# Two layers of attention and token-mixing MLP on one core: a PSUM tile of its own for each of the three accumulators of a pair

## The chip, the cores and the metric

The kernel runs on one core of one Trainium2 chip. The metric is the device time of one execution in microseconds (us). Three runs of the kernel before gave 2514.11, 2517.06 and 2518.97 us; their median is 2517.06 us.

## The reference, cut to what matters

Two kinds of layer alternate, each twice, on x of 2048 tokens by 512 channels, all in float32:

```python
x = x + _A_ref(_layernorm(x), wq, wk, wv, wo)     # attention, 32 query heads, one key and value head
x = x + _B_ref(_layernorm(x), w1, b1, w2, b2)     # token mixing
...
def _B_ref(x, w1, b1, w2, b2):
    h = _layernorm(x)                             # (S, D)
    u = _gelu(einsum("bsd,sf->bdf", h, w1) + b1)  # (D, F), F = 1792
    y = einsum("bdf,fs->bds", u, w2) + b2         # (D, S)
    return y.transpose                            # (S, D)
```

The change touches only the second matrix product of the last token-mixing layer: y = W2ᵀu for all 2048 tokens, with a sum over the 1792 rows of w2.

## The kernel before

Every product is made in float32 precision out of three passes: each operand is split in a high part (a rounded copy, made by ScalarE at L1465 in `split`) and a low part (the rest, made by VectorE at L1466), and TensorE multiplies high by high, high by low and low by high, in this order (`split_terms`). So the first and second matmul of a triple read only the high part of the left operand, the third needs the low part.

The program is one stream: attention of layer 0, mixing of layer 0, attention of layer 1, mixing of layer 1. In the last stage, `pairs` (from the last product with w1 to the end), the output is made in 8 pairs of token tiles, a pair being two tiles of 128 tokens. u lies in SBUF as 14 tiles of 128 rows. For two pairs (`WHOLE_PAIR`) the product is made plainly: four quarter blocks of 7 × 3 matmuls of 512 columns. For the other six (`ENTRY_PAIR` once, then `PAIR` five times) a 2 by 2 block product is made with seven block products instead of eight (a scheme after Strassen and Winograd). Each block is 7 × 3 matmuls of 256 columns (L1579 in `block`). The left operand of a block is a 128-column block of w2 or a sum of such blocks, made by VectorE (`outer_sum`, L1507 and L1512); the right operand is a half of u (B11, B21, B22) or a sum of halves (T1 to T4) made earlier.

The seven blocks of a pair, by their place j, with the accumulator (X, Z or Y) each one adds to and the parts of x that are updated ("evicted") when it ends:

```python
PAIR = (
    ("A11", "B11", "X", True, ("11b",)), ("A12", "B21", "Z", True, ("11",)),
    ("S2", "T2", "X", False, ("12b",)), ("S1", "T1", "Y", True, ("22b",)),
    ("S3", "T3", "X", False, ("22",)), ("S4", "B22", "Y", False, ("12",)),
    ("A22", "T4", "X", False, ("21b",)),
)
```

So X takes blocks 0, 2, 4 and 6, Z takes block 1 alone, Y takes blocks 3 and 5. An accumulator goes on growing after it has been read: X is read after block 0, then block 2 adds to it. The eviction is one VectorE instruction that reads PSUM and adds into x in SBUF: L1588 (with the bias) or L1592 (without).

PSUM has eight banks of 512 float32 a partition. The pool "sc" has three tiles of two banks (`bank2`); "ac0" and "ac1" are one bank each (`bank`). Before the change, a pair takes one two-bank tile, X is its first half and Z its second half, that is, the bank beside it; Y is a single bank. The framework records waits by tile: an instruction that writes a part of a tile waits for the earlier readers of that tile, whichever part they read.

The order of instructions is the order in which the code is written, engine by engine. For block n of the whole stage, `split_pair(n + 2)` comes first (ScalarE's high part, VectorE's low part, of the left operand for two blocks later), then `beside` (outer sums of the next pair from place 3 on, the loads of w2 for a later pair on SP's queue at place 5; in the entry pair the split of T1 at places 0 to 3), then the matmuls of block n, then its eviction. So in VectorE's queue each eviction of block n stands behind the low part for block n + 2 and behind one outer sum.

Of the kernel before, what the change touches and what calls it, by code (L numbers as in the profile page):

```python
# [68 lines left out]
NPAIR, NWHOLE = NKT // 2, 2  # L69
# [20 lines left out]
def kernel(  # L90
# [26 lines left out]
    def bank2(name):  # L117
        return ps.tile([P, 2, QB], F32, tag="sc", bufs=3, name=name)

    def bank(i, name):  # L120
        return ps.tile([P, QB], F32, tag=f"ac{i % 2}", name=name)
# [973 lines left out]
    class Mixer:  # L1095
# [442 lines left out]
        def pairs(self):  # L1538

            n = 0  # L1540
            for q, table in enumerate(PAIRS):
                both = bank2(f"py_{q}")
                banks = {"X": both[:, 0], "Z": both[:, 1], "Y": bank(q, f"pyy_{q}")}
                for j, entry in enumerate(table):
                    self.split_pair(n + 2)
                    self.beside(q, j, n)
                    self.block(q, n, banks[entry[2]], *entry)
                    n += 1
# [354 lines left out]
```

## Time and profile before

| what | value |
|---|---|
| runs | 2514.11, 2517.06, 2518.97 us; median 2517.06 us |
| the profiled execution | 2514.75 us, span of the trace 2513.0 us |
| VectorE busy | 1623.0 us, 65% of the span |
| ScalarE busy | 2127.2 us, 85% |
| DMA | mean 57 GB/s |
| stage `pairs` | first matmul of L1579 at 2352.7 us, last eviction at 2509.33 us |
| first block of the entry pair | starts at 2391.61 us |

Times in the trace are us from the start of the span. A row of the timeline has the start, the length, the engine, the line, the operation, what it writes and what it reads, how many equal instructions in a row it holds and, in brackets, how long the engine sat idle before it and what ended that idle time. PE is TensorE's matmul, PEld its weight load, DVE is VectorE, ACT is ScalarE. The tile of X and Z is named py, that of Y pyy; rA holds w2's blocks, rS a sum of them, w a split left operand; t, u, kst and qs hold right operands.

### The profile page before, as it was taken

To read this page: it belongs to the slowest core of one execution; us is meant where nothing else is said; L and a number is where in the kernel's file an instruction comes from. 1 tells how busy PE (TensorE), PEld (TensorE's weight loads), DVE (VectorE), ACT (ScalarE), POOL (GpSimd) and SP (SyncE) were. 2 spreads that over 40 slices of the span, in tenths; PEclk is the share of its full clock that TensorE was granted. 3 is DMA by queue.
4 is the path that set the end of the run, shared out by engine and by line. 5 is a ranking of instruction groups with operands and counts; after the bars stand their busy time and mean duration, and the time that the engine had idled before them with its cause. 6 is when DMAs were issued, how large, how long until landed. Compare 5 with 4: busy or idle time off the path is not lost. (4 is left out here: it accounts for less than half of the span.)

```text
span 2513.0 us, 42927 instructions
## 1 busy us (share of the span) xinstructions
PE 2488.0 (99%) x16536; PEld 1252.8 (50%) x16536; DVE 1623.0 (65%) x2587; ACT 2127.2 (85%) x2390; POOL 147.5 (6%) x235
## 2 busy tenths in 40 slices
PE   9999999999999999999999999999999999999998
PEld 6444344444444444588863443444444444446888
DVE  6565566667766776564545664666677667765776
ACT  6999999999999999653349999999999999995532
POOL 5000000000000000141000000000000000002200
PEclk9999999999999999999999999999999999999999
DMA  3221201110111111144413211111111111102442
GB/s 116 75 66 41 65 29 39 33 40 31 39 31 39 32 40 31 44 113 147 125 57 118 67 39 48 32 40 31 39 32 42 33 40 32 40 27 68 116 141 65
DMA packets 168684, 143.63 MB, mean 57 GB/s; under 512 B 17650, under 2 KB 132368, under 8 KB 167952
## 3 DMA queue, kind: packets, MB, share of 16 engines
q1 hardware_dynamic: 168464, 140.72, 18.9%
q8 instruction: 135, 2.21, 0.4%
q14 instruction: 85, 0.70, 0.1%
HBM read 97.67 MB, written 26.22 MB: 49 GB/s over the span
## 5 line engine op out<-in xcount | busy, mean ns | idle before, releaser
L939 ACT ACTIVATE p<-sc 128x1024 f32<-128x1024 f32 x1444 | 1405.7, 1049 | 62.6 <-PE sc L929 61.4
L937 DVE COPY p<-sc 128x1024 f32<-128x1024 f32 x604 | 739.1, 1224 | 523.3 <-PE sc L929 438.4
L945 PE MATMUL acc<-p,vaug 128*32 128x512 f32 x8192 | 1000.1, 599 | 0.4 <-DVE q L548 0.4
L929 PE MATMUL sc<-qs,kst 51*128 51x512 f32 x4096 | 683.9, 432 | 6.8 <-SPq L647 2.6
L939 ACT ACTIVATE p<-p 128x1024 f32<-128x1024 f32 x604 | 655.8, 1086 | 14.2 <-DVE p L937 9.2
L929 PEld LDWEIGHTS sc<-qs,kst 51*128 51x128 f32 x4096 | 338.2, 184 | 559.5 <-ACT p L939 387.4
L945 PEld LDWEIGHTS acc<-p,vaug 128*32 128x32 f32 x8192 | 219.0, 109 | 489.4 <-issue 473.1
L1224 PE MATMUL pu<-hb,w 128*128 128x512 f32 x792 | 209.4, 406 | 0.0
L1224 PEld LDWEIGHTS pu<-hb,w 128*128 128x128 f32 x792 | 140.9, 188 | 57.6 <-issue 32.0
L1211 POOL TENSOR_TENSOR w<-w1r,w 128x256 fp32r<-128x256 f32 x86 | 69.4, 815 | 1581.9 <-ACT w L1209 1581.2
L1627 PE MATMUL py<-u,w 128*128 128x512 f32 x672 | 154.8, 390 | 0.0
L1627 PEld LDWEIGHTS py<-u,w 128*128 128x128 f32 x672 | 125.7, 188 | 26.1
L865 DVE RECIPROCAL o<-o 128x128 f32<-128x128 f32 x120 | 113.3, 944 | 9.0 <-DMA o<-ev 9.0
L906 PE MATMUL po<-wo,hl 128*128 128x512 f32 x360 | 100.2, 412 | 0.1
L1615 ACT CAST w<-w2r 128x896 fp32r<-128x896 f32 x32 | 30.0, 943 | 76.8 <-PE py L1627 69.5
L1465 ACT CAST w<-rA 128x896 fp32r<-128x896 f32 x44 | 41.3, 942 | 62.3 <-PE py L1579 44.4
L847 DVE COPY ev<-acc 128x512 f32<-128x512 f32 x64 | 43.7, 682 | 62.7 <-PE acc L945 62.7
L435 PE MATMUL pq<-hT,wq 128*128 128x512 f32 x312 | 81.1, 403 | 0.0
L906 PEld LDWEIGHTS po<-wo,hl 128*128 128x128 f32 x360 | 62.6, 188 | 33.7 <-issue 15.9
L1224 PE MATMUL pu_l<-hb,w 128*128 128x512 f32 x336 | 77.1, 389 | 0.0
L1209 ACT CAST w<-w1r 128x256 fp32r<-128x256 f32 x86 | 34.3, 406 | 48.0 <-PE pu_l L1224 16.6
L1616 DVE TENSOR_TENSOR w<-w2r,w 128x896 fp32r<-128x896 f32 x32 | 37.1, 1159 | 52.2 <-ACT w L1615 52.2
(224 smaller groups left out, 1628.1 us busy)
## 6 DMA issues: line engine op xcount, KB each, us to landing
w1r<-in_B_w_dram SPq DMA_DIRECT2D x224, 128.0 KB
qs<-qd SPq DMA_DIRECT2D x384, 64.0 KB
qd<-q SPq DMA_DIRECT2D x64, 256.0 KB
o<-ev SPq DMA_DIRECT2D x128, 128.0 KB
w2r<-in_B_w_dram SPq DMA_DIRECT2D x32, 448.0 KB
rA<-in_B_w_dram SPq DMA_DIRECT2D x32, 448.0 KB
x<-in_A_x_dram SPq DMA_DIRECT2D x16, 256.0 KB
hd<-hT SPq DMA_DIRECT2D x2, 2048.0 KB
```

Source lines behind the costliest of these rows:

```text
L435: yield nc.tensor.matmul(out, a, c, start=(k == 0), stop=(k == len(terms) - 1))
L847: nc.vector.tensor_copy(ev, acc)
L865: nc.vector.reciprocal(o[:, 1, c], o[:, 1, c])
L906: nc.tensor.matmul(po, a, c, start=(k == 0), stop=(k == 3 * len(parts) - 1))
L929: nc.tensor.matmul(sc[:, j, :], kst[kt // 4][rows, kt % 4 * P : (kt % 4 + 1) * P], qs[i % NQ][rows, j0 // 2, :], start=True, stop=True,)
L937: nc.vector.tensor_copy(pt, sc)
L939: nc.scalar.activation(pt, sc, AF.Exp, scale=0.25)
L945: nc.tensor.matmul(self.acc[i][c : c + 32, :], vaug[:, kt].rearrange("p d k -> p (d k)"), pt[:, j, :], start=(kt == 0), stop=(kt == NKT - ...
L1211: eng.tensor_tensor(w[:, 1], raw, f32(w[:, 0]), op=ALU.subtract)
L1224: nc.tensor.matmul(pu, a, c, start=(start and k == 0), stop=(stop and k == 5))
L1465: nc.scalar.copy(out[:, 0], src)
L1627: nc.tensor.matmul(py, a, d, start=(c == 0 and f == 0 and k == 0), stop=(c == 1 and f == NFH - 1 and k == 2),)
```

## The change

```diff
             for q, table in enumerate(PAIRS):
-                both = bank2(f"py_{q}")
-                banks = {"X": both[:, 0], "Z": both[:, 1], "Y": bank(q, f"pyy_{q}")}
+                banks = {key: bank2(f"py{key}_{q}")[:, 0] for key in ("X", "Z")[: 1 + (q >= NWHOLE)]}
+                banks["Y"] = bank(q, f"pyY_{q}")
```

X and Z each get a two-bank tile from the same pool of three and use the first bank of it. The two plain pairs, which have no Z, take one such tile as before. In the six other pairs two of the three tiles are in use at a time instead of one. As built, Z lies in bank 2 in all six pairs and X in banks 6, 4, 6, 4, 6, 4; before, X lay in banks 6, 2, 4, 6, 2, 4 and Z in the bank above each. Y keeps banks 0 and 1 in turn. No instruction is added, removed or moved on any engine; what differs is which semaphores some matmuls wait for, and up to what count.

On TensorE, in the pair with q = 4, the end of block 0 (left operand w_22, into X) and the start of block 1 (w_23, into Z) stand so before; a row is a line of code, an operation, the tile written, the tiles read, the size, and the semaphores waited for (DVE is VectorE's, Activation ScalarE's):

```order
L1579 MATMUL py_25115<-u_10_24020,w_22_25053 128x256 x3
L1579 MATMUL py_25115<-u_12_24022,w_22_25053 128x256 x3
L1579 MATMUL py_25115<-u_1_24011,w_23_25088 128x256 [waits DVE_49,Activation_49]
L1579 MATMUL py_25115<-u_1_24011,w_23_25088 128x256 x2
L1579 MATMUL py_25115<-u_3_24013,w_23_25088 128x256 x3
```

The same place after the change:

```order
L1579 MATMUL pyX_25117<-u_10_24020,w_22_25055 128x256 x3
L1579 MATMUL pyX_25117<-u_12_24022,w_22_25055 128x256 x3
L1579 MATMUL pyZ_25118<-u_1_24011,w_23_25090 128x256 [waits Activation_49]
L1579 MATMUL pyZ_25118<-u_1_24011,w_23_25090 128x256
L1579 MATMUL pyZ_25118<-u_1_24011,w_23_25090 128x256 [waits DVE_49]
L1579 MATMUL pyZ_25118<-u_3_24013,w_23_25090 128x256 x3
```

Block 1's first matmul no longer waits for VectorE; its third matmul, the first that reads a low part, does.

On TensorE, in the same pair, the end of block 2 (w_24, into X) and the start of block 3 (w_25, into Y) before:

```order
L1579 MATMUL py_25115<-t_5_24610,w_24_25117 128x256 x3
L1579 MATMUL py_25115<-t_6_24652,w_24_25117 128x256 x3
L1579 MATMUL pyy_25116<-u_0_24010,w_25_25142 128x256 [waits Activation_49]
L1579 MATMUL pyy_25116<-u_0_24010,w_25_25142 128x256 x2
L1579 MATMUL pyy_25116<-u_2_24012,w_25_25142 128x256 x3
```

And after:

```order
L1579 MATMUL pyX_25117<-t_5_24610,w_24_25120 128x256 x3
L1579 MATMUL pyX_25117<-t_6_24652,w_24_25120 128x256 x3
L1579 MATMUL pyY_25119<-u_0_24010,w_25_25145 128x256 [waits Activation_49]
L1579 MATMUL pyY_25119<-u_0_24010,w_25_25145 128x256
L1579 MATMUL pyY_25119<-u_0_24010,w_25_25145 128x256 [waits DVE_49]
L1579 MATMUL pyY_25119<-u_2_24012,w_25_25145 128x256 x3
```

Block 3 has gained a wait of its own for the low part of w_25. Before, that low part was covered by the wait at the start of block 2, which was for the eviction of block 1 (behind that low part in VectorE's queue); after, block 2's first matmul still waits for VectorE, in a row that reads alike, but up to a lower count: that of the eviction of block 0.

## The prediction

> **What bounds the kernel now.** I read the page first: which engine is busy, and how much of the span is left for a gain at all.
>
> ```profile
> span 2513.0 us, 42927 instructions
> PE 2488.0 (99%) x16536; PEld 1252.8 (50%) x16536; DVE 1623.0 (65%) x2587; ACT 2127.2 (85%) x2390; POOL 147.5 (6%) x235
> ```
>
> TensorE is busy for 99% of the span; it is the bound, and what can be won without taking matmuls away is the time in which it stands still. Next I asked for the one line that the change touches, L1579, and what its engine waited for before it.
>
> ```profile
> its engine sat idle before it (us, times) until:
>   issue: 8.9, 11
>   DVE x L1588: 5.7, 6
>   DVE x L1592: 3.6, 6
> ```
>
> The matmuls stood still 6 times until an eviction at L1588 had ended and 6 times until one at L1592 had: twelve waits, two in each of the six pairs that have a Z. (The 8.9 us of "issue" are weight loads standing beside the same waits, not further time.) To see where they lie I read the timeline of one whole pair, q = 4.
>
> ```profile
> 2430.61 1.09 DVE L1466 TENSOR_TENSOR w<-rA,w 128x896 fp32r<-128x896 f32 x1
> ...
> 2431.89 2.68 PE L1579 MATMUL py<-u,w 128*128 128x256 f32 x21
> 2432.74 0.48 DVE L1588 SCALAR_TENSOR_TENSOR x<-py,b2c,x 128x256 f32<-128x256 f32 x1
> 2433.14 1.08 DVE L1466 TENSOR_TENSOR w<-rA,w 128x896 fp32r<-128x896 f32 x1
> 2434.61 0.48 DVE L1588 SCALAR_TENSOR_TENSOR x<-py,b2c,x 128x256 f32<-128x256 f32 x1 [0.39 <-PE py L1579]
> 2434.67 0.94 ACT L1465 CAST w<-rS 128x896 fp32r<-128x896 f32 x1 [1.59 <-PE py L1579]
> 2435.24 2.76 PE L1579 MATMUL py<-u,w 128*128 128x256 f32 x21 [0.67 <-DVE x L1588]
> 2435.64 1.09 DVE L1466 TENSOR_TENSOR w<-rS,w 128x896 fp32r<-128x896 f32 x1 [0.54 <-ACT w L1465]
> 2438.04 0.42 DVE L1592 TENSOR_TENSOR x<-x,py 128x256 f32<-128x256 f32 x1 [1.31 <-PE py L1579]
> 2438.61 2.73 PE L1579 MATMUL py<-t,w 128*128 128x256 f32 x21 [0.61 <-DVE x L1592]
> 2441.18 2.68 PE L1579 MATMUL pyy<-u,w 128*128 128x256 f32 x21
> 2444.36 0.48 DVE L1588 SCALAR_TENSOR_TENSOR x<-pyy,b2c,x 128x256 f32<-128x256 f32 x1
> 2446.20 2.68 PE L1579 MATMUL pyy<-u,w 128*128 128x256 f32 x21
> 2446.88 0.41 DVE L1592 TENSOR_TENSOR x<-x,py 128x256 f32<-128x256 f32 x1
> 2448.72 1.59 PE L1579 MATMUL py<-kst,w 128*128 128x256 f32 x12
> 2451.22 2.68 PE L1579 MATMUL py<-u,w 128*128 128x256 f32 x21
> ```
>
> Blocks 0, 1 and 2 start at 2431.89, 2435.24 and 2438.61, block 3 (into Y) at 2441.18, the next pair at 2451.22. Between block 0 and block 1, and between block 1 and block 2, TensorE waits for an eviction; from block 3 on each starts as the one before ends, although evictions go on there too, because X and Y take turns.
>
> **The change part by part.**
>
> *The length of a block without a wait.* Blocks 3 to 6 take 2451.22 − 2441.18 = 10.04 us, 2.51 us each. I use starts, not the lengths in the rows: 2.68 us for a block that is followed after 2.51 us has its pipeline's end drawn in. For the same reason the idle times (0.67 and 0.61 us) are shorter than what a wait costs.
>
> *The first wait, block 1 on X's eviction, removed.* Block 1 could start at 2431.89 + 2.51 = 2434.40. The eviction starts 0.21 us after that, runs 0.48 us, and block 1 starts 0.15 us after its end, at 2435.24: 0.84 us lost. Block 1 writes into Z, which nobody is reading; only the shared tile makes it wait.
>
> *The second wait, block 2 on Z's eviction, removed.* Block 2 could start at 2435.24 + 2.51 = 2437.75, and starts at 2438.61: 0.86 us. Block 2 itself lasts 2.57 us from start to start, 0.06 us more than one that follows without a break. Together the three blocks take 9.29 us where 3 × 2.51 = 7.53 us would do: 1.76 us a pair. The idle rows say that the other pairs are alike: 3.6 us over 6 waits at L1592 is 0.60 each, and 5.7 us at L1588, less the longest (2.37 us, below), is 0.67 each over 5. So the five pairs of kind PAIR give 5 × 1.76 = 8.8 us.
>
> *The entry pair.* It waits longer:
>
> ```profile
> 2391.61 2.68 PE L1579 MATMUL py<-u,w 128*128 128x256 f32 x21
> 2394.37 1.08 DVE L1466 TENSOR_TENSOR w<-rA,w 128x896 fp32r<-128x896 f32 x1
> 2395.37 0.75 DVE L1466 TENSOR_TENSOR u<-t,u 128x256 fp32r<-128x256 f32 x2
> 2396.04 0.48 DVE L1588 SCALAR_TENSOR_TENSOR x<-py,b2c,x 128x256 f32<-128x256 f32 x1
> 2396.66 2.75 PE L1579 MATMUL py<-u,w 128*128 128x256 f32 x21 [2.37 <-DVE x L1588]
> 2402.59 2.68 PE L1579 MATMUL pyy<-u,w 128*128 128x256 f32 x21
> ```
>
> Here X's eviction starts only at 2396.04, since a low part and the split of T1 stand ahead of it on VectorE. Blocks 0 to 2 take 2402.59 − 2391.61 = 10.98 us, 3.45 us over 7.53. Without the first wait block 1 starts at 2394.12 and block 2 could start at 2396.63; it must still wait for X's eviction, 2396.04 + 0.48 + 0.15 = 2396.67, so 0.04 us of the gain stays behind. Of this pair I count 3.4 us.
>
> *What becomes late next.* Block 2 keeps its true wait, for the eviction of X after block 0. In the pair above that ended 2434.61 + 0.48 − 2431.89 = 3.20 us after block 0's start, 3.35 with the 0.15 to the next matmul; block 2 comes 5.02 us after it. Slack 1.67 us: hidden behind block 1. The waits added, on the third matmul of blocks 1 and 3 for a low part: that of block 1 ends at 2430.61 + 1.09 = 2431.70, before block 0 begins; that of block 3 (2435.64 + 1.09) ends 4.84 us after block 0's start, follows a cast at 2434.67 which waits for block 0's end and no later one, and is needed after 7.5 us. What such a wait costs when it is already met no row isolates; block 0 has one on its third matmul now, and its eviction starts 2434.61 − 2431.89 = 2.72 us after its start, against 2438.04 − 2435.24 = 2.80 for block 1, which has none. I take 0, and ± 0.02 us each, ± 0.2 us in all twelve, as bounds. Behind those waits only TensorE's own next matmuls are queued. Block 6 waits for block 4's eviction, which ends at 2447.29, 1.43 us before block 6 starts; block 5 for block 3's, which ends at 2444.84, 1.36 us before.
>
> *VectorE's share.* It gets the same work in less time.
>
> ```profile
> core 0: us, PE busy (x) PEld busy (x) DVE busy (x) ACT busy (x) POOL busy (x), PEclk, DMA share, GB/s
> 2391.40:2412.60 21.20, 18.22 (x149) 17.82 (x148) 18.21 (x28) 8.73 (x14) 0.00 (x0) 1.00 0.58 163
> 2431.90:2451.30 19.40, 18.12 (x150) 17.77 (x149) 14.67 (x19) 6.59 (x7) 0.00 (x0) 1.00 0.43 125
> ```
>
> A pair shrinks to 7 × 2.51 = 17.6 us. VectorE has 14.67 us in it: room. In the entry pair it has 18.21 us, more than 17.6 (durations of neighbours overlap by up to 0.1 us, so truly a little less): evictions will run late there, by up to 0.6 us, against slacks of 1.3 to 1.7, and the next pair has 2.9 us to make it up. I take no stall from it, and as a bound that half of this pair's gain, 1.7 us, is given back. The weights come at 125 GB/s with the DMA engines 43% busy; 10% more a second does not fill them. ScalarE has 6.59 us.
>
> *The end.* After the last matmul the eviction and the store remain as they are:
>
> ```profile
> 2509.33 0.48 DVE L1588 SCALAR_TENSOR_TENSOR x<-py,b2c,x 128x256 f32<-128x256 f32 x1 [2.08 <-PE py L1579]
> ```
>
> From this last eviction to the span's end 3.7 us stay, and so does everything ahead of 2391.61 us.
>
> *The sum.* 8.8 + 3.4 = 12.2 us off the profiled execution: 2514.75 − 12.2 = 2502.6, with a span near 2500.8. The profiled execution lies 2.3 us under the median of the three runs; against that, 2517.06 − 12.2 = 2504.9 us, my forecast. Bounds of the gain: 12.2 + 0.2 = 12.4 above, 12.2 − 0.2 − 1.7 = 10.3 below.
>
> Could an unbroken block be shorter than 2.51 us, so that more is to be won? The two plain pairs have matmuls of twice the width:
>
> ```profile
> 2372.10 9.96 PE L1579 MATMUL py<-u,w 128*128 128x512 f32 x42
> 2381.90 9.87 PE L1579 MATMUL pyy<-u,w 128*128 128x512 f32 x42
> ```
>
> There 42 matmuls of 512 columns take 9.80 us, 0.233 us each; half of that, 0.117 us for 256 columns, makes 2.45 us for 21, at the same granted clock of 1.00. I keep to 2.51, which blocks of this very kind show. The Trainium skill ("TensorE: Matmul & The Clock Gate", section "Back-to-back issue gap") gives 262 cycles for an isolated matmul of 256 columns, an estimated 2.29 us for 21 of them at its full clock of 2.4 GHz. The trace does not agree with it for this stream, in which each matmul has a weight load of its own. By that pace the waits would be estimated at 2.42 us a pair and 4.11 in the entry pair, 16.2 us in all.
>
> **The rivals.**
>
> *Only half goes.* Were the eviction of X after block 0 later than reckoned, block 2 would stall on it in place of Z's. Then about 0.86 us a pair stays, 12.2 − 6 × 0.86 = 7.0 us are won: 2510.1 us. For it: the entry pair is 0.04 us from this. Against: 1.67 us of slack in the other five.
>
> *Nothing comes of it.* The time is given back at another wait, later in each pair (blocks 4 to 6) or on a new tile: Z now draws on the same three tiles as X. That gives 2517.1 us. Against: Z's own first matmul waits for ScalarE alone, and X, in banks 6 and 4 by turns, never takes the tile that X had in the pair before.
>
> *Slower: VectorE becomes the bound.* Its place is the queue from block 3 on, where a low part, an outer sum and an eviction come in every 2.51 us. If its instructions grew longer once TensorE writes without a break, evictions would fall behind and blocks 4, 5, 6 would stall. From 17.6 us of VectorE work a pair, 20% over 14.67, the gain shrinks; from 19.3 us, 32% over, it turns. At 40%, 20.5 us a pair, the five pairs would lose 5 × 1.2 = 6 us: 2523 us. Against: the eviction at 2432.74 took 0.48 us with TensorE at work, the one at 2434.61 took 0.48 with TensorE standing.
>
> *Blocks that are faster too.* Were the 42 blocks held back by these waits in a way that no idle row shows, they could come down to the 2.45 us of the plain pairs: 42 × 0.06 = 2.5 us more, 14.7 us in all, 2502.4 us. Against: blocks 3 to 6 follow each other without a wait now and take 2.51. The isolated pace stated by the Trainium skill ("TensorE: Matmul & The Clock Gate", "Back-to-back issue gap") would carry this further, to an estimated 2500.9 us.
>
> **How the numbers follow.** Forecast 0.86, half 0.06, nothing 0.04, slower 0.03, faster blocks 0.01. The range follows the forecast's bounds, laid on the lowest and highest run: 2514.11 − 12.4 = 2501.7 and 2518.97 − 10.3 = 2508.7; the other cases, 0.14 together, may be left out. A measurement of this kernel can tell about 0.2%, 5 us, from no change. Faster by more than that: the forecast, the faster blocks, and half of the half case, 0.90; within it: the other half and "nothing", 0.07; slower: 0.03.
>
> **What would show it.** In the profile after: blocks 0 to 2 start 2.5 us apart in every pair; the idle rows of L1579 name L1588 and L1592 no more, but for some tenths of a us in the entry pair; a PAIR takes 17.6 us; VectorE's busy time is the same. I am wrong if a stall stands at block 2 (half), at blocks 4 to 6 with longer idle times until L1588 or L1592 (VectorE), or if unbroken blocks take other than 2.51 us.

## The result, and the profile after

The changed kernel took 2502.63 us (median of five runs, 2501.36 to 2506.12) against 2515.78 us for the kernel before (five runs, 2514.11 to 2518.97): a ratio of 0.995 with a 95% interval from 0.9936 to 0.9965, that is 13.15 us by the medians and 8.8 to 16.1 us by the interval. The forecast was 12.2 us. The profiled execution took 2502.08 us.

The page after, and under it the answer for line L1579 with its idle times:

```profile
span 2500.3 us, 42921 instructions
PE 2484.6 (99%) x16536; PEld 1251.9 (50%) x16536; DVE 1622.2 (65%) x2587; ACT 2127.2 (85%) x2390; POOL 148.2 (6%) x235
```

```profile
its engine sat idle before it (us, times) until:
who waited for it (us, times):
...
```

The counts of TensorE and VectorE are the same; the span is 12.7 us shorter. Under the heading of idle times there is nothing left: in the whole stage no matmul of L1579 finds its engine idle. The timeline of the pair q = 4, which the prediction showed before the change:

```profile
2426.22 2.68 PE L1579 MATMUL pyX<-u,w 128*128 128x256 f32 x21
2428.74 2.68 PE L1579 MATMUL pyZ<-u,w 128*128 128x256 f32 x21
2428.94 0.48 DVE L1588 SCALAR_TENSOR_TENSOR x<-pyX,b2c,x 128x256 f32<-128x256 f32 x1 [0.39 <-PE pyX L1579]
...
2431.26 2.65 PE L1579 MATMUL pyX<-t,w 128*128 128x256 f32 x21
2431.46 0.42 DVE L1592 TENSOR_TENSOR x<-x,pyZ 128x256 f32<-128x256 f32 x1 [0.40 <-PE pyZ L1579]
...
2433.75 2.68 PE L1579 MATMUL pyY<-u,w 128*128 128x256 f32 x21
...
2443.80 2.68 PE L1579 MATMUL pyX<-u,w 128*128 128x256 f32 x21
```

Block 1 starts 2.52 us after block 0, while X's eviction has not even begun (2428.94, 0.20 us later); block 2 starts before Z's eviction. Blocks 0 to 2 take 2433.75 − 2426.22 = 7.53 us in place of 9.29, the pair 17.58 in place of 19.33. In the entry pair:

```profile
2391.04 2.68 PE L1579 MATMUL pyX<-u,w 128*128 128x256 f32 x21
...
2393.56 2.68 PE L1579 MATMUL pyZ<-u,w 128*128 128x256 f32 x21
...
2395.48 0.48 DVE L1588 SCALAR_TENSOR_TENSOR x<-pyX,b2c,x 128x256 f32<-128x256 f32 x1
...
2396.10 2.74 PE L1579 MATMUL pyX<-t,w 128*128 128x256 f32 x21
...
2398.68 2.68 PE L1579 MATMUL pyY<-u,w 128*128 128x256 f32 x21
```

7.64 us in place of 10.98. And the end of the stage:

```profile
2496.66 0.48 DVE L1588 SCALAR_TENSOR_TENSOR x<-pyX,b2c,x 128x256 f32<-128x256 f32 x1 [2.08 <-PE pyX L1579]
```

From the first narrow block (the first with 256 columns) to the start of the last eviction the stage lasts 2496.66 − 2391.04 = 105.62 us; before it was 2509.33 − 2391.61 = 117.72. So 12.10 us of the 12.7 come from this stage. The other 0.57 us lie ahead of it, where the change does nothing: the narrow blocks begin at 2391.04 instead of 2391.61.

### The profile page after: what moved, and what is told of

Same layout as the page of the kernel before. It is cut to its first block, busy times and chain, and to the rows that moved or that the text cites. A ratio compares the mean times of both kernels' runs of the same rounds, so it can differ in the third digit from the quotient of the medians.

```text
span 2500.3 us, 42921 instructions
## 1 busy us (share of the span) xinstructions
PE 2484.6 (99%) x16536; PEld 1251.9 (50%) x16536; DVE 1622.2 (65%) x2587; ACT 2127.2 (85%) x2390; POOL 148.2 (6%) x235
```

## The experiments

Single runs of one kernel differ by up to 6.8 us (the kernel before, beside one set of experiments: 2513.22 to 2519.99). In the profiled executions this lies ahead of the stage: z_on_y below reaches it at 2395.02 us, z_upper at 2391.16, and both then need 105.6 us for it. So beside the medians the table gives the length of this stage, taken as above from the one profile of each kernel; the kernels in which nothing stands still agree in it to 0.02 us. Each interval is against runs of the kernel before that were made beside that kernel; their medians lie between 2514.74 and 2515.94 us.

| kernel | median, us | ratio to before, 95% interval | stage, us |
|---|---|---|---|
| before | 2515.78 | | 117.72 |
| after | 2502.63 | 0.9936 to 0.9965 | 105.62 |
| z_on_y | 2504.16 | 0.9935 to 0.9962 | 105.64 |
| z_upper | 2502.70 | 0.9935 to 0.9962 | 105.63 |
| first_kept | 2511.36 | 0.9975 to 0.9993 | 112.65 |
| second_kept | 2510.40 | 0.9970 to 0.9988 | 113.60 |
| second_in_pairs | 2506.59 | 0.9959 to 0.9981 | 110.07 |
| second_again | 2513.83 (one run) | | 113.63 |
| before_late | 2519.29 | 1.0005 to 1.0023 | 122.31 |
| after_late | 2502.32 | 0.9934 to 0.9961 | 105.62 |
| after_later | 2510.76 | 0.9972 to 0.9991 | 112.31 |

The theory: X and Z sharing one tile made two waits a pair that no data asked for, each exposed on TensorE with its own price. The rivals: the banks themselves matter; the two waits hide one another; the gap is TensorE's own turn-around; VectorE has no room.

**Z in Y's bank (z_on_y).** Nothing gets a tile more than before; Z goes into Y's tile, which it leaves before Y opens.

```diff
-                banks = {key: bank2(f"py{key}_{q}")[:, 0] for key in ("X", "Z")[: 1 + (q >= NWHOLE)]}
-                banks["Y"] = bank(q, f"pyY_{q}")
+                banks = {"X": bank2(f"pyX_{q}")[:, 0], "Y": bank(q, f"pyY_{q}")}
+                banks["Z"] = banks["Y"]
```

> Z has no tile of its own: block 1 goes into Y's bank, X keeps a tile for itself. Theory (the time came from two false waits, made by X and Z sharing a tile; any partner that is not read while its neighbour is written will do): Z's eviction runs during block 2, before block 3 opens Y, so nothing stands still and the time is that of the kernel after, 2502.6 us, within 2 us. Rival (each accumulator needs a bank or tile of its own): block 3 now waits for Z's eviction, about 0.9 us in each of six pairs are given back, about 2508 us.

The pair q = 4 in its timeline (pyY is Z in the first and third row, Y in the last):

```profile
2432.74 2.68 PE L1579 MATMUL pyY<-u,w 128*128 128x256 f32 x21
...
2435.27 2.65 PE L1579 MATMUL pyX<-t,w 128*128 128x256 f32 x21
2435.47 0.42 DVE L1592 TENSOR_TENSOR x<-x,pyY 128x256 f32<-128x256 f32 x1 [0.40 <-PE pyY L1579]
...
2437.75 2.68 PE L1579 MATMUL pyY<-u,w 128*128 128x256 f32 x21
```

Z's eviction ends at 2435.89, 1.86 us before block 3 opens the same bank. The stage is 105.64 us, the same as with three tiles. The rival falls: a tile for each accumulator is not needed; it is enough that the tile being read is not the one written next.

**Z in the second bank of its tile (z_upper).**

```diff
-                banks = {key: bank2(f"py{key}_{q}")[:, 0] for key in ("X", "Z")[: 1 + (q >= NWHOLE)]}
+                banks = {key: bank2(f"py{key}_{q}") for key in ("X", "Z")[: 1 + (q >= NWHOLE)]}
+                banks = {key: two_[:, int(key == "Z")] for key, two_ in banks.items()}
```

> As the kernel after, but Z lies in the second bank of its own two-bank tile, an odd bank as it was before the change. Theory (only the recorded waits matter): 2502.6 us, within 2 us. Rival (part of the gain comes from the banks that X and Z were moved to): up to half of it, 6 us, comes back, about 2509 us.

2502.70 us, stage 105.63: whether Z lies in an even or an odd bank makes no difference here. X right beside Z in one pair of banks, as before, but without the waits, was not tried.

**Only the first wait kept (first_kept).** From the kernel before, with the shared tile: Z's eviction is written behind the matmuls of block 2.

```diff
...
+            if key == "Z":
+                self.late = q, out, outs
+                return
+            if late:
+                self.evict(*late)
+            self.evict(q, out, outs, right, left)
...
```

> The kernel before with X and Z in one tile; Z's eviction is written behind the matmuls of block 2, so that block 2 no longer waits for it, while block 1 still waits for X's eviction. Theory (each wait costs its own stall, 0.84 and 0.86 + 0.06 us, and they add up): about 0.9 us less in each of six pairs than before, 5.5 us in all, about 2510.3 us; the stalls until L1588's instruction stay at 5.7 us, those until L1592's go. Rival (the two waits hide one another, so that taking one away only lengthens the other): no change, 2515.8 us.

Evictions with the bias stand at L1598 here. The idle times, then the pair q = 4:

```profile
its engine sat idle before it (us, times) until:
  DVE x L1598: 5.8, 6
```

```profile
2434.19 2.74 PE L1581 MATMUL py<-u,w 128*128 128x256 f32 x21 [0.67 <-DVE x L1598]
...
2436.77 2.66 PE L1581 MATMUL py<-t,w 128*128 128x256 f32 x21
...
2439.27 2.68 PE L1581 MATMUL pyy<-u,w 128*128 128x256 f32 x21
```

The first wait is as it was, 5.8 us of idle time before six matmuls; the second is gone. The stage loses 117.72 − 112.65 = 5.07 us, 0.85 a pair, where 5.5 was expected: the 0.06 us by which a block after a wait is longer do not go, they move from block 2 to block 1 (2.58 us). The change took 7.03 us more than this from the stage, which is the first wait's part: 0.90 us in each of the five pairs of kind PAIR (8.43 against 7.53 for blocks 0 to 2) and 2.54 us in the entry pair (10.18 against 7.64). Whether the two add up is seen only when the second is kept alone.

**Only the second wait kept (second_kept, second_again, second_in_pairs).** From the kernel after: behind Z's eviction, VectorE copies one element of T2 onto itself, so that block 2 must wait.

```diff
                     self.block(q, n, banks[entry[2]], *entry)
+                    if entry[2] == "Z":
+                        one = self.operand("T2", 0)[:1, 0, :1]
+                        nc.vector.tensor_copy(one, f32(one))
```

> The kernel after, with the second wait put back: behind Z's eviction VectorE copies one element of block 2's right operand onto itself, so block 2 waits for that, block 1 for nothing. Theory: a stall of 0.9 us and of the small copy (0.1 to 0.2 us) in front of block 2 in six pairs, 6 to 7 us over the kernel after, about 2509 us. Rival (the waits hide one another): all 12 to 13 us come back, about 2515.8 us, or none, 2502.6 us.

The pair q = 4:

```profile
2435.19 0.42 DVE L1595 TENSOR_TENSOR x<-x,pyZ 128x256 f32<-128x256 f32 x1 [0.40 <-PE pyZ L1582]
2435.53 0.13 DVE L1550 CAST t<-t 1x1 fp32r<-1x1 f32 x1
...
2435.81 2.71 PE L1582 MATMUL pyX<-t,w 128*128 128x256 f32 x21 [0.66 <-DVE t L1550]
```

The stall is back at block 2 and nowhere else, and block 2 starts 0.15 us after the end of the copy (2435.66), as blocks 1 and 2 started 0.15 us after the evictions. But the stage is 7.98 us longer than after, not 6 to 7. The entry pair accounts for it: its blocks 0 to 2 take 11.19 us there instead of 7.64, 3.55 us more, and block 2 alone takes 4.07 us. The windows around it (columns as in the prediction):

```profile
2392.80:2397.40 4.60, 2.71 (x23) 2.51 (x22) 4.60 (x11) 3.10 (x6) 0.00 (x0) 1.00 0.80 230
2397.40:2401.50 4.10, 4.07 (x21) 4.10 (x22) 1.55 (x3) 0.00 (x0) 0.00 (x0) 0.58 0.69 203
```

After 1.9 us of idle time, block 2 ran at a granted clock of 0.58. Two more runs ask whether that was chance: the same kernel once more, and one with the copy left out of the entry pair (`and q > NWHOLE`).

> second_kept once more, to see whether the granted clock of 0.58 in block 2 of the entry pair comes back. If the idle time ahead of it (1.9 us) brings it about, block 2 lasts 4.07 us again and the stage 113.6 us from its first narrow block to its last eviction; if it was a chance of that execution, block 2 lasts 2.57 us and the stage 112.1 us.

> As second_kept, but with no copy in the entry pair. Theory: the second wait costs 0.87 us in each of five pairs, 4.3 us over the kernel after, about 2507 us, and no block of the entry pair is longer than in the kernel after (7.64 us for blocks 0 to 2). Rival (what second_kept lost beyond 5.5 us was lost in all six pairs alike): about 6.5 us, 2509 us.

second_again showed it again, a little later in the block and on into the next one:

```profile
2397.00:2401.60 4.60, 2.99 (x25) 2.79 (x24) 4.60 (x9) 3.07 (x6) 0.00 (x0) 1.00 0.86 244
2401.60:2405.50 3.90, 3.58 (x22) 3.61 (x23) 1.84 (x5) 0.03 (x1) 0.00 (x0) 0.71 0.66 189
2405.50:2408.00 2.50, 2.50 (x18) 2.50 (x18) 1.78 (x3) 1.25 (x2) 0.00 (x0) 0.77 0.32 96
```

Blocks 2 and 3 last 3.58 and 3.02 us, 1.5 us more together than 2.57 and 2.51; the stage is 113.63 us. With no copy in the entry pair its blocks 0 to 2 take 7.66 us and the stage 110.07: 4.45 us over after, 0.89 in each of five pairs, of which the copy is 0.05 (it ends at 2435.66, the eviction at 2435.61). So the second wait alone costs 0.84 us in such a pair, and with the first wait's 0.90 this makes 1.74 of the 1.76 us: there neither hides the other. The entry pair of second_kept loses 3.55 us in two parts: block 2 starts 2.06 us later (4.60 us after block 1 in place of 2.54), because VectorE, busy for all 4.60 us of the first window above, comes late to the eviction and the copy, and it then lasts 1.49 us longer at the lower clock. In that pair the waits do hide one another in part: 2.54 us with the first alone, 2.06 with the second alone before the clock falls, but only 3.34 with both.

**A later eviction (before_late, after_late, after_later).** Needless VectorE instructions on tiles that are no longer used, ahead of X's eviction after block 0 in five pairs: four of them, or ten.

```diff
+            if q > NWHOLE and left == "A11":
+                for i in range(4):
+                    nc.vector.tensor_tensor(self.t1[i % 3], self.t1[3 + i % 2], self.t1[5], op=ALU.subtract)
             done = set()
             for to in outs:
```

> The kernel before with four needless VectorE instructions of 128x256 (0.34 us apart, about 1.35 us) ahead of X's eviction after block 0, in the five pairs behind the entry pair. VectorE idles 0.39 us there, so the eviction comes about 1.0 us later. Theory (block 1 stands still until this eviction): 1.0 us more in each of five pairs, 5 us over the kernel before, about 2521 us. Rival (the stall between block 0 and block 1 is TensorE's own turn-around and not the eviction): 2515.8 us.

In before_late the pair q = 4 shows the four instructions, the eviction (here L1591) and block 1:

```profile
2432.77 2.68 PE L1579 MATMUL py<-u,w 128*128 128x256 f32 x21
...
2435.01 1.42 DVE L1585 TENSOR_TENSOR t<-t,t 128x256 f32<-128x256 f32 x4
...
2436.36 0.47 DVE L1591 SCALAR_TENSOR_TENSOR x<-py,b2c,x 128x256 f32<-128x256 f32 x1
...
2436.98 2.75 PE L1579 MATMUL py<-u,w 128*128 128x256 f32 x21 [1.53 <-DVE x L1591]
```

Block 1 starts 0.15 us after the eviction again, 4.21 us after block 0 in place of 3.35; the stage grows by 4.59 us, 1.17 in the first of the five pairs and about 0.85 in each of the others. The gap is the eviction and moves with it; it is no turn-around of TensorE's.

> The kernel after with the same four needless instructions at the same place. Theory (X's eviction now has 1.67 us of slack before block 2): the 1.0 us are hidden, 2502.6 us, within 2 us. Rival (VectorE is close to being the bound, or has no slack): 1.0 to 1.35 us more in each of five pairs, 2507.6 to 2509.4 us.

The same four instructions in the changed kernel:

```profile
2429.59 1.43 DVE L1585 TENSOR_TENSOR t<-t,t 128x256 f32<-128x256 f32 x4
2429.87 2.68 PE L1579 MATMUL pyZ<-u,w 128*128 128x256 f32 x21
...
2430.93 0.48 DVE L1591 SCALAR_TENSOR_TENSOR x<-pyX,b2c,x 128x256 f32<-128x256 f32 x1
...
2432.39 2.65 PE L1579 MATMUL pyX<-t,w 128*128 128x256 f32 x21
```

The eviction ends at 2431.41, 0.98 us before block 2. The stage is 105.62 us, the same to the last digit: what cost 4.59 us before is free after.

> The kernel after with ten such instructions, 3.4 us, so that X's eviction comes about 3.0 us later. Theory: 1.67 us of that are hidden and block 2 stands still for the other 1.3 us in each of five pairs, 6.7 us over the kernel after, about 2509.3 us; the idle rows name L1588's instruction again, at block 2 alone. Rival (no true wait is left at block 2): 2502.6 us. Rival (VectorE's 14.6 + 3.4 = 18.0 us a pair becomes the bound of 17.55): 0.45 us a pair, 2.3 us, about 2505 us.

```profile
2432.14 3.44 DVE L1585 TENSOR_TENSOR t<-t,t 128x256 f32<-128x256 f32 x10
...
2432.41 2.68 PE L1579 MATMUL pyZ<-u,w 128*128 128x256 f32 x21
...
2435.13 0.94 ACT L1465 CAST w<-rA 128x896 fp32r<-128x896 f32 x1 [1.52 <-PE pyZ L1579]
2435.49 0.48 DVE L1591 SCALAR_TENSOR_TENSOR x<-pyX,b2c,x 128x256 f32<-128x256 f32 x1
...
2436.12 2.73 PE L1579 MATMUL pyX<-t,w 128*128 128x256 f32 x21 [1.02 <-ACT w L1465]
```

With ten, the slack is used up and block 2 stands still in the five pairs; the stage grows by 6.69 us, as expected 6.7. VectorE being full would have given 2.3. Note the releaser: the row names ScalarE's cast at 2435.13, which ended last by the profile (2436.07). But that cast makes the left operand for a later block; the start at 2436.12 is 0.15 us after the eviction's end at 2435.97, as in every other such row.

## Why the prediction was right

*The block's length.* 2.51 us was taken from blocks 3 to 6; all seven take it now on average (17.58 us for seven; single blocks of the five pairs last 2.46 to 2.52 us, blocks 3 to 6 before the change just so). The shorter pace weighed beside it, 2.45 us from the plain pairs, is not the pace of any pair. The Trainium skill ("TensorE: Matmul & The Clock Gate", "Back-to-back issue gap") states its 262 cycles for an isolated matmul, an estimated 2.29 us for 21 of them. The trace does not agree with it for this stream: at a granted clock of 1.00, 21 matmuls with a weight load each take 2.51 us with no wait left.

*The waits.* 1.76 us a pair was forecast, 9.29 − 7.53 = 1.76 us was measured. The experiments split it: about 0.85 us from the second wait, the rest from the first.

*The entry pair.* 3.4 us was forecast, 10.98 − 7.64 = 3.34 came. X's eviction ended at 2395.96 and block 2 started 0.14 us later, 2.54 us after block 1: the 0.04 us expected there showed as 0.03, with 0.07 us on block 2 itself.

*The added waits.* 0 was taken. Block 1, now with a wait on its third matmul, takes 2.52 us, block 4, without one, 2.51.

*VectorE.* The entry pair was the doubtful place.

```profile
2390.90:2408.60 17.70, 17.70 (x149) 17.62 (x148) 17.63 (x28) 8.75 (x14) 0.00 (x0) 1.00 0.69 192
2426.10:2443.70 17.60, 17.60 (x150) 17.60 (x149) 14.62 (x19) 6.59 (x7) 0.00 (x0) 1.00 0.48 137
```

VectorE is busy for 17.63 of 17.70 us there, and TensorE loses no more than the 0.10 us named above: the slack of 1.3 to 1.7 us was enough. In the other pairs it has 3 us to spare. Its busy time in a pair is 14.62 us where it was 14.67, so its instructions grew no longer beside an unbroken TensorE, which the slower rival needed.

*The end.* From the last eviction to the end of the span it is 3.64 us (3.67 before).

*The sum.* 12.2 us forecast, 12.10 in the stage. The forecast of 2504.9 us stood on a median of three runs, 2517.06; with five it is 2515.78, which is most of the difference to the 2502.63 measured. The rest, like the 0.57 us ahead of the stage, is within the spread between executions. By the time alone the rival of faster blocks (2502.4 us) lies nearer than the forecast; that it is not what happened is shown by the 2.51 us of the blocks and the 12.10 us of the stage.

## What to carry to other kernels

When an engine waits for an instruction that reads something it is not about to touch, look at how the waits are recorded: two accumulators in one tile wait for each other's readers, and giving them different tiles (or a partner that is out of use at the time) costs no instruction. Price such a wait by the starts of the blocks around it, not by the idle times: here the twelve idle times were 9.3 us and the waits cost 12.1. Then ask for the slack of the wait that stays, and test it with a dose: 1.4 us of needless work ahead of the eviction in each of five pairs cost 4.6 us in all before and nothing after.

## What the runs showed of the hardware that was not expected

A short idle time of TensorE can be followed by a lower clock, and it need not. In second_kept, 1.92 us of idle time ahead of block 2 of the entry pair was followed by 4.1 us at a mean granted clock of 0.58, and in second_again 1.93 us by windows at 0.71 and 0.77; each cost 1.5 us. In the kernel before, a longer idle time of 2.37 us, one block earlier in the same pair, was followed by no lower clock. So the length of the idle time alone does not decide.

What fits is where the idle time lies. In second_kept the granted clock is 0.50 for one stretch of 3.41 us, and the stretches at full clock before and behind it are 1095.68 and 105.81 us, 321 and 31 times 3.413. Counted in such steps, the idle time lies whole in the step just ahead of the low one (TensorE is busy for 1.49 of 3.41 us):

```profile
2394.30:2397.71 3.41, 1.49 (x13) 1.32 (x12) 3.41 (x9) 1.88 (x5) 0.00 (x0) 1.00 0.66 200
2397.71:2401.13 3.42, 3.42 (x18) 3.42 (x17) 1.24 (x3) 0.00 (x0) 0.00 (x0) 0.50 0.71 209
```

It is the same in second_again: 1.93 us idle between 2399.81 and 2403.22, then 0.50 up to 2406.64. In the kernel before, counted on from the change of its clock at 1303.61 us, a boundary falls into the idle time and leaves 1.58 us of it in one step and 0.79 us in the next:

```profile
2392.46:2395.87 3.41, 1.83 (x16) 1.62 (x14) 3.38 (x6) 2.45 (x6) 0.00 (x0) 1.00 1.15 302
2395.87:2399.29 3.42, 2.63 (x21) 2.58 (x21) 2.31 (x5) 0.05 (x1) 0.00 (x0) 1.00 0.63 176
2399.29:2402.70 3.41, 2.80 (x24) 2.71 (x23) 2.19 (x4) 1.55 (x3) 0.00 (x0) 1.00 0.45 125
```

The most idle time that one step held among the narrow blocks with no lower clock behind it is 1.84 us (before_late, 2394.51 to 2397.92). This account fits all eleven profiles, but no run moved an idle time across a boundary to test it. Nor is the amount a fixed one: near 1300 us, in an earlier stage, 1.41 us in a step was followed by 0.50 (after_later, 1294.71 to 1298.12). The same steps make up most of what z_on_y and z_upper differ by ahead of the stage: z_on_y ran at 0.50 for 6.82 us from 47.91 and again from 1300.60, z_upper for 3.41 us from 46.68 and from 1299.37; at half clock that is 3.4 of the 3.86 us.
